# Which engine folds the attention output, and in how many pieces, in a fused attention, Fourier mixing and MLP kernel on one core

## The chip, the cores and the metric

The kernel runs on one core of one Trainium2 chip. The metric is the device time of one execution in microseconds (us), as the median of three runs. The core's engines are TensorE (PE in the trace; PEld are its weight loads), VectorE (DVE), ScalarE (ACT), GpSimd (POOL) and SyncE (SP), which issues the DMAs. Each works through its own queue in order and waits on semaphores for the others.

## What is computed

Four batches of 768 tokens pass through three blocks. The first is a gated linear attention with 8 heads of 48; its output, 768 x 384 per batch, gets a two-dimensional Fourier transform, whose real part is added, a normalisation and an MLP; then come a token-mixing MLP and a second channel MLP.

```python
# attention, per batch and head
for t in range(S):
    S_re, S_im = ar * S_re - ai * S_im + kv, ar * S_im + ai * S_re
    y[:, :, t] = einsum('bhd,bhde->bhe', q[:, :, t], S_re)
# block 1
mixed = real(fft(fft(x, axis=1), axis=2))
u = x + mixed
un = (u - mean(u)) / sqrt(var(u) + 1e-6)
x = u + relu(un @ w_ch1) @ w_ch2
# block 2
u = x + (relu(x.T @ w_tok1) @ w_tok2).T
out = u + relu(u @ w_ch1) @ w_ch2
```

## The kernel before

**Two streams.** The work on a batch has a chain part (the attention, `stage1`, and the Fourier mixing, `stage2`, with many short operations on all engines) and a dense part (the two MLPs and the token mixing: matmuls of 128 x 128 by 128 x 384). The kernel writes the chain of batch b+1 beside the dense part of batch b. A scheduler puts both into one order per engine when the kernel is built, by priorities (`RANK`) and its own estimate of times; on the chip these orders are fixed. Only the first batch's chain (beside which the weights are converted, L191 to L206) and the last two batches' dense part have no such partner.

**The end of the attention.** `stage1` works through 8 chunks of 96 tokens. For each, TensorE does L753 (scores), L768 and L769 (state), L802 and L808 (output), and ScalarE writes the chunk's 96 columns of the tile `xT` (L810). L808 and L753 read the tile `qkt`, of the pool tag "qk", which has one buffer of 12288 columns.

**The folds.** `stage2` folds `xT`, 112 x 4 x 768, for a Fourier transform that uses symmetries. L982 adds and subtracts columns n and 384 + n (xm and xp), so a piece of columns needs chunk k and chunk k + 4. L988 adds and subtracts the halves of xm and xp (four results xd). L999 adds or subtracts each xd and its mirror image, for four types `ty` of transform and two halves r (eight results fd); it needs whole rows of 384. In batches 2 to 4 (b = 1 to 3) xm, xp, xd and fd lie in `ws`, which is again of the tag "qk"; in the first batch xm, xp and xd lie elsewhere. Then ScalarE copies the edge columns (L1006), TensorE multiplies by cosines and sines (L1022, two matmul records for each in the trace), ScalarE copies to Z (L1024), TensorE does the second transform (L1033), and the rows are joined, normalised and transposed (L1080, L1085 to L1114, L906 to L910).

**Who folds.** `XP` gives the pieces (start, width) of a batch: four of 96 in the first batch, one of 288 and one of 96 in the others. `PD` names the xd results that GpSimd makes (in later batches xd[1][1]), `PF` the fd results that GpSimd makes in later batches (type 2, both halves). xp is always GpSimd's, the rest VectorE's. In front of a later batch's folds stand, in VectorE's queue, the last L760 and the dense part's operations; between them the scheduler puts dense ones: L932 (the MLP's rectified hidden, from PSUM) and L945 (adds the MLP's output to u, from PSUM). TensorE's dense matmuls, L926 (first MLP matrix) and L942 (second), write PSUM tiles of tag "l", of which there are three: a tile is free again when L932 or L945 has read it. One quarter of an MLP is six groups of nine L926, then six groups of nine L942.

Of the kernel before, what the change touches and what calls it, by code (L numbers as in the profile page):

```python
# [34 lines left out]
AH = 4  # L35
KS, EN = 5, 3
OFF = ((2, 3), 1, 0)
XP = [((0, 96), (96, 96), (192, 96), (288, 96))] + [((0, 288), (288, 96))] * 4
NR = [((0, 192),)] * 5
KT, PF, PD = (0, 1), ((2, 0), (2, 1)), (((1, 0), (1, 1)), ((1, 1),))  # L40
O = (0, 1, 0)
HOLD = mybir.DependencyInfo(mybir.DependencyClass.NoSync, mybir.DependencyReason.SCHED_ONLY)
CHK_A, CHK_E = 6.0e4, 1.0e-7
# [10 lines left out]
def attn_fft_mixer_kernel(ctx: ExitStack, tc: tile.TileContext, aL, xL, vL, wL, qN, kN, vN, arN, aiN,  # L54
# [18 lines left out]
    ve, se, ge = Prio(nc.vector, "v"), Prio(nc.scalar, "v"), Prio(nc.gpsimd, "v")  # L73
# [18 lines left out]
    def alloc(tag, shape, dt=F32, name=None):  # L92
        n = 1
        for x in shape[1:]:
            n *= x
        t = pool.tile([128, SIZE[tag]], dt, tag=tag, bufs=BUFS[tag], name=name or tag)
        return shaped(t[0:shape[0], 0:n], shape)
# [37 lines left out]
    xT = pool.tile([112, 4, S], F32, name="xT")  # L135
# [29 lines left out]
    def after(x, y):  # L165
        tc.add_manual_dep(x.ins, y.ins.name, HOLD, reason="order of the streams")
# [138 lines left out]
    def warm(n, x):  # L305

        ps = palloc("l", [128, 512])
        for _ in range(n):
            te.matmul(out=ps[:, 0:x.shape[1]], lhsT=ident[0:x.shape[0], :], rhs=x)
# [644 lines left out]
    def stage2(b):  # L954
        space = alloc("qk", [128, 12288], name="ws")
        def part(name, pat=None, **kw):
            o, n = WSP[name]
            v = space[:, o:o + n]
            return v.rearrange(pat, **kw) if pat else v
# [6 lines left out]
        if b == 0:  # L966

            xm, xp = (alloc("h", [112, 4, 384], name="xf") for _ in range(2))
            xd = alloc("h", [112, 4, 384], name="xd")
            xd = [[xd[:, 0:2], xd[:, 2:4]], [alloc("tmp", [112, 2, 384], name="xd") for _ in range(2)]]  # L970
        else:
            xf = part("xf", "p (a b) -> p a b", a=8)[0:112]
            xm, xp = xf[:, 0:4, :], xf[:, 4:8, :]
            xd = part("xd", "p (s r a b) -> p s r a b", s=2, r=2, a=2)[0:112]
            xd = [[xd[:, s, r] for r in range(2)] for s in range(2)]
        fd = part("fd", "p (t r a b) -> p t r a b", t=4, r=2, a=2)[0:112]
        Z = part("Z", "p (a b) -> p a b", a=8)
        for k, (o, n) in enumerate(XP[b]):
            n += o
            an = None if b or AN[k] is None else free[AN[k]]  # L980
            for s, x, op in ((0, xm, ALU.subtract), (1, xp, ALU.add)):
                x1 = (ge if s else ve).tensor_tensor(out=x[:, :, o:n], in0=xT[:, :, o:n], in1=xT[:, :, 384 + o:384 + n], op=op)  # L982
                if an is not None:
                    after(x1, an)
                if b == 0 and k == 3 and s == 0:
                    warm(1, xm[:, 0, :])
                for r, op2 in enumerate((ALU.add, ALU.subtract)):
                    x1 = (ge if (s, r) in PD[b > 0] else ve).tensor_tensor(out=xd[s][r][:, :, o:n], in0=x[:, 0:2, o:n], in1=x[:, 2:4, o:n], op=op2)  # L988
                    if an is not None:
                        after(x1, an)  # L990
                    if b == 0 and k == 3 and s == 0:
                        warm(1, xd[0][r][:, 0, :])

        kinds = ((0, 0, ALU.subtract, 0, 191), (1, 0, ALU.add, 1, 192), (2, 1, ALU.add, 0, 192), (3, 1, ALU.subtract, 1, 191))
        for n0, n1 in NR[b]:
            for ty, s, op, f0, f1 in kinds:
                lo, hi, sh = max(n0, f0, 1), min(n1, f1, 191) + 1, ty % 2
                for r in range(2):
                    x = (ge if (ty, r) in PF and b else ve).tensor_tensor(out=fd[:, ty, r, :, lo - sh:hi - sh], in0=xd[s][r][:, :, lo:hi],  # L999
                                                                in1=xd[s][r][:, :, 384 - lo:384 - hi:-1], op=op)  # L1000
                    if b == 0 and ty < 2:
                        warm(1, fd[:, ty, r, 0, 1:191])
                for n in (0, 192):
                    if n0 <= n <= n1 and f0 <= n <= f1:
                        for r in range(2):
                            se.copy(out=fd[:, ty, r, :, n - sh:n - sh + 1], in_=xd[s][r][:, :, n:n + 1])  # L1006
# [9 lines left out]
        for kt in KT:  # L1016
            for ty in range(4):
                n0, n = 128 * kt, ZK[ty][kt]
# [37 lines left out]
        for i in range(3):  # L1056
# [19 lines left out]
            for half in range(2):  # L1076
# [10 lines left out]
                lo, hi = (1, 2) if half == 0 else (2, 1)  # L1087
# [111 lines left out]
    def chain(b):  # L1199
        stage1(b)  # L1200
        return stage2(b)
# [28 lines left out]
    with tc.If(fv != 0):  # L1230
        with tc.For_i(0, B, 1) as b:
            fallback(b)
            u, norm = stage2(B)
            t = transposed(u, norm, "s")
            dense2(B, u, *dense1(B, u, *t), row=b)
# [111 lines left out]
```

## Time and profile before

| | |
|---|---|
| median of three runs (lowest to highest) | 1103.9 us (1103.21 to 1104.33) |
| profiled execution | 1103.4 us, of which its span 1101.6 us |
| mean granted clock of TensorE over the span | 0.955 |
| busy: TensorE, VectorE, ScalarE, GpSimd | 985.5, 784.3, 506.2, 387.3 us |

The span reaches from the first to the last instruction of the profiled execution; all places in it are us from its start. A granted clock of 1.00 is 2.4 GHz, 0.50 is 1.2 GHz. A row of the timeline merges instructions of one kind that follow each other (x27); its time reaches from the first one's start to the last one's end, and since an instruction starts shortly before the one ahead of it ends, the distance from start to start is less than a duration. In square brackets stands how long the engine was idle before the row and what ended that.

### The profile page before, as it was taken

What the parts mean: (1) busy time and instruction counts of PE and PEld (TensorE: products, weight loads), DVE (VectorE), ACT (ScalarE), POOL (GpSimd) and SP (SyncE); (2) the same over time, 40 slices, a digit from 0 to 9 for tenths busy, and PEclk for the clock granted to TensorE, in tenths of its full rate; (3) what the DMA queues carried; (4) which work ended last, traced back from release to release, by engine and by line L of the source; (5) the groups of instructions that cost most, each with busy time, mean ns of one, the idle gap of its engine ahead of it and who ended that gap; (6) DMA issues with size and microseconds to landing.
All of it is one profiled execution on the core that took longest, in us unless ns stands there. A gap on an engine that the chain in (4) does not pass through costs nothing.

```text
span 1101.6 us, 21033 instructions
## 1 busy us (share of the span) xinstructions
PE 985.5 (89%) x7314; PEld 923.1 (84%) x7314; DVE 784.3 (71%) x2115; ACT 506.2 (46%) x1393; POOL 387.3 (35%) x520
## 2 busy tenths in 40 slices
PE   1368887999889999799998999999986999999997
PEld 0237775989788888699998899999976999999997
DVE  6986987999999668999767879985555433433332
ACT  6753355777876225867423567751124112121111
POOL 6643985573576444223226312211432002000000
PEclk9987797999999998899998999999988999999999
DMA  6137954686758664355565336655412433443432
GB/s 215 45 82 179 293 176 154 209 283 194 231 179 278 194 178 135 99 168 185 179 160 172 112 112 193 205 161 146 139 48 66 151 115 129 158 151 130 165 101 74
DMA packets 101536, 174.65 MB, mean 159 GB/s; under 512 B 11056, under 2 KB 61104, under 8 KB 100912
## 3 DMA queue, kind: packets, MB, share of 16 engines
q1 hardware_dynamic: 101424, 173.24, 51.1%
q8 instruction: 60, 0.98, 0.4%
q14 instruction: 52, 0.43, 0.1%
HBM read 133.88 MB, written 39.32 MB: 157 GB/s over the span
## 4 chain that ended last, share of the span: by engine, by line
PE 65%; DVE 10%; DMA 2%; ACT 1%; issue 1%; POOL 1%; SPq 0%; POOLq 0%; DVEq 0%; ACTq 0%
PE l L942 24%; PE l L926 22%; PE s L753 3%; PE s L642 2%; PE s L1033 2%; PE s L1022 2%; PE s L802 2%; DMA cvt<-wL 2%; PE s L808 1%; PE s L1147 1%; DVE ws L982 1%; PE s L1165 1%; PE s L768 1%; DVE cvt L199 1%; PE s L906 1%
## 5 line engine op out<-in xcount | busy, mean ns | idle before, releaser
L942 PE MATMUL l<-w,h 128*128 128x384 f32 x1728 | 332.5, 345 | 12.1 <-DVE h L932 8.4
L926 PE MATMUL l<-th,w 128*128 128x384 f32 x1152 | 314.4, 342 | 5.1 <-DVE h L932 2.6
L942 PEld LDWEIGHTS l<-w,h 128*128 128x128 f32 x1728 | 304.4, 192 | 16.8 <-DVE h L932 11.6
L926 PEld LDWEIGHTS l<-th,w 128*128 128x128 f32 x1152 | 210.8, 190 | 9.1 <-DVE h L932 4.1
L930 ACT ACTIVATE h<-l 128x384 fp32r<-128x384 f32 x192 | 94.0, 490 | 225.3 <-PE l L926 224.8
L926 PE MATMUL l<-tl,w 128*128 128x384 f32 x576 | 195.3, 339 | 0.0
L932 DVE SCALAR_TENSOR_TENSOR h<-l,h 128x384 fp32r<-128x384 f32 x192 | 106.2, 553 | 88.3 <-ACT h L930 87.9
L945 DVE TENSOR_TENSOR u<-u,l 128x384 f32<-128x384 f32 x192 | 105.4, 550 | 76.0 <-PE l L942 75.1
L926 PEld LDWEIGHTS l<-tl,w 128*128 128x128 f32 x576 | 109.1, 189 | 0.4 <-issue 0.2
L196 POOL TENSOR_TENSOR cvt<-cvt 128x384 int32<-128x384 int32 x56 | 64.8, 1163 | 38.2 <-DVE cvt L194 9.4
L466 PE MATMUL s<-misc,y 128*112 128x128 f32 x96 | 22.1, 377 | 52.1 <-DVE y L444 48.6
L753 PE MATMUL s<-qkt 112*96 112x96 f32 x512 | 59.7, 267 | 8.0 <-DVE sc L760 7.9
L466 PEld LDWEIGHTS s<-misc,y 128*112 128x112 f32 x96 | 14.5, 181 | 61.9 <-issue 27.3
L753 PEld LDWEIGHTS s<-qkt 112*96 112x96 f32 x512 | 53.4, 177 | 11.1 <-DVE sc L760 8.7
L786 POOL TENSOR_TENSOR yc<-Aa,gm 48x384 f32<-48x384 f32 x18 | 21.0, 1165 | 100.8 <-DVE Aa L779 100.8
L206 POOL TENSOR_TENSOR w<-cvt,w 128x384 fp32r<-128x384 f32 x44 | 51.1, 1170 | 10.5 <-ACT w L205 7.0
L199 DVE SCALAR_TENSOR_TENSOR cvt<-cvt 128x384 int32<-128x384 int32 x56 | 48.8, 878 | 7.0 <-POOL cvt L196 6.8
L1132 POOL TENSOR_TENSOR xl<-u,xh 128x384 fp32r<-128x384 f32 x18 | 17.9, 1004 | 101.1 <-ACT xh L1131 101.1
L571 POOL TENSOR_TENSOR tm<-tm 128x144 f32<-128x144 f32 (+1 forms) x51 | 26.6, 523 | 73.7 <-ACT tm L570 73.7
L642 PE MATMUL s<-misc,y 128*112 128x128 f32 x288 | 45.7, 275 | 1.5 <-DVE y L626 1.0
L615 DVE TENSOR_TENSOR p<-p,A 128x144 f32<-128x144 f32 x144 | 44.7, 310 | 2.0
L589 POOL TENSOR_TENSOR A<-raw,tm 128x144 f32<-128x144 f32 (+1 forms) x51 | 26.1, 513 | 56.0 <-DVE tm L587 29.4
(232 smaller groups left out, 1905.3 us busy)
## 6 DMA issues: line engine op xcount, KB each, us to landing
w<-wscr SPq DMA_DIRECT2D x180, 384.0 KB, 3.5
cvt<-wL SPq DMA_DIRECT2D x56, 384.0 KB, 4.7
wscr<-w SPq DMA_DIRECT2D x44, 384.0 KB, 3.2
Kn<-kn SPq DMA_DIRECT2D x64, 192.0 KB, 3.8
kn<-y SPq DMA_DIRECT2D x96, 96.0 KB, 2.7
raw<-aL SPq DMA_DIRECT2D x48, 144.0 KB, 3.0
xx<-xL SPq DMA_DIRECT2D x48, 144.0 KB, 3.2
V<-vL SPq DMA_DIRECT2D x32, 144.0 KB, 3.3
```

Of the source, the lines that this page charges most:

```text
L196: x = ge.tensor_tensor(out=a, in0=a, in1=lo, op=ALU.add)
L199: rest(ve.scalar_tensor_tensor(out=a, in0=hi, scalar=-0x80000000, in1=a, op0=ALU.bitwise_and, op1=ALU.bitwise_or))
L206: ge.tensor_tensor(out=parts[:, 1, :], in0=a.bitcast(F32), in1=r32(parts[:, 0, :]), op=ALU.subtract)
L466: te.transpose(ps[:, j, :], y[:, j, 0:112], ident)
L615: ve.tensor_tensor(out=cur, in0=prev, in1=A[:, j, 0:3, :], op=ALU.mult)
L642: te.transpose(ps[:, j, :], y[:, j, 0:112], ident)
L753: te.matmul(out=ps[:, j, :], lhsT=K[:, hc, :], rhs=Q[:, hc, :])
L926: te.matmul(out=ps, lhsT=w1[:, wi, kt * 128:kt * 128 + 128], rhs=x[g][:, kt, :], start=(n == 0), stop=(n == 8))
L930: x = se.activation(out=hi, in_=ps, func=ACTF.Relu)
L932: ve.scalar_tensor_tensor(out=h[:, 1, g * 384:g * 384 + 384], in0=ps, scalar=0.0, in1=r32(hi), op0=ALU.max, op1=ALU.subtract)
L942: te.matmul(out=ps, lhsT=hs[m][:, hi, tt * 128:tt * 128 + 128], rhs=w2[:, wi, :], start=(n == 0), stop=(n == 8))
L945: ve.tensor_tensor(out=u[tt], in0=u[tt], in1=ps, op=ALU.add)
```

## The change

All batches get four pieces of 96 columns. GpSimd makes xp, and the xd results that `PD` names, only for the first three of them (k < 3), in the first batch as well; the fourth piece is VectorE's alone. `PF` is gone: all L999 run on VectorE.

```diff
--- before.py
+++ after.py
@@ -35,9 +35,9 @@
 AH = 4
 KS, EN = 5, 3
 OFF = ((2, 3), 1, 0)
-XP = [((0, 96), (96, 96), (192, 96), (288, 96))] + [((0, 288), (288, 96))] * 4
+XP = [((0, 96), (96, 96), (192, 96), (288, 96))] * 5
 NR = [((0, 192),)] * 5
-KT, PF, PD = (0, 1), ((2, 0), (2, 1)), (((1, 0), (1, 1)), ((1, 1),))
+KT, PD = (0, 1), (((1, 0), (1, 1)), ((1, 1),))
 O = (0, 1, 0)
 HOLD = mybir.DependencyInfo(mybir.DependencyClass.NoSync, mybir.DependencyReason.SCHED_ONLY)
 CHK_A, CHK_E = 6.0e4, 1.0e-7
@@ -979,13 +979,13 @@
             n += o
             an = None if b or AN[k] is None else free[AN[k]]
             for s, x, op in ((0, xm, ALU.subtract), (1, xp, ALU.add)):
-                x1 = (ge if s else ve).tensor_tensor(out=x[:, :, o:n], in0=xT[:, :, o:n], in1=xT[:, :, 384 + o:384 + n], op=op)
+                x1 = (ge if s and k < 3 else ve).tensor_tensor(out=x[:, :, o:n], in0=xT[:, :, o:n], in1=xT[:, :, 384 + o:384 + n], op=op)
                 if an is not None:
                     after(x1, an)
                 if b == 0 and k == 3 and s == 0:
                     warm(1, xm[:, 0, :])
                 for r, op2 in enumerate((ALU.add, ALU.subtract)):
-                    x1 = (ge if (s, r) in PD[b > 0] else ve).tensor_tensor(out=xd[s][r][:, :, o:n], in0=x[:, 0:2, o:n], in1=x[:, 2:4, o:n], op=op2)
+                    x1 = (ge if k < 3 and (s, r) in PD[b > 0] else ve).tensor_tensor(out=xd[s][r][:, :, o:n], in0=x[:, 0:2, o:n], in1=x[:, 2:4, o:n], op=op2)
                     if an is not None:
                         after(x1, an)
                     if b == 0 and k == 3 and s == 0:
@@ -996,7 +996,7 @@
             for ty, s, op, f0, f1 in kinds:
                 lo, hi, sh = max(n0, f0, 1), min(n1, f1, 191) + 1, ty % 2
                 for r in range(2):
-                    x = (ge if (ty, r) in PF and b else ve).tensor_tensor(out=fd[:, ty, r, :, lo - sh:hi - sh], in0=xd[s][r][:, :, lo:hi],
+                    x = ve.tensor_tensor(out=fd[:, ty, r, :, lo - sh:hi - sh], in0=xd[s][r][:, :, lo:hi],
                                                                 in1=xd[s][r][:, :, 384 - lo:384 - hi:-1], op=op)
                     if b == 0 and ty < 2:
                         warm(1, fd[:, ty, r, 0, 1:191])
```

In the order that the scheduler makes, three places show it. First VectorE in the fourth batch (b = 3), beside the dense part of the third: L760 ends the attention, u_65.. are the token tiles of the dense part. Before:

```order
L760 TENSOR_TENSOR sc<-s,misc 96x384 x2
L932 SCALAR_TENSOR_TENSOR h<-l,h 128x384
L982 TENSOR_TENSOR ws<-xT 112x4x288
L982 TENSOR_TENSOR ws<-xT 112x4x96
L988 TENSOR_TENSOR ws<-ws 112x2x288 x2
L945 TENSOR_TENSOR u_6503<-u_6503,l 128x384
L988 TENSOR_TENSOR ws<-ws 112x2x96 x2
L988 TENSOR_TENSOR ws<-ws 112x2x288
L945 TENSOR_TENSOR u_6504<-u_6504,l 128x384
L988 TENSOR_TENSOR ws<-ws 112x2x96
L999 TENSOR_TENSOR ws<-ws 112x2x191 x4
```

With the change:

```order
L760 TENSOR_TENSOR sc<-s,misc 96x384
L945 TENSOR_TENSOR u_6516<-u_6516,l 128x384
L760 TENSOR_TENSOR sc<-s,misc 96x384
L982 TENSOR_TENSOR ws<-xT 112x4x96 x3
L988 TENSOR_TENSOR ws<-ws 112x2x96 x2
L945 TENSOR_TENSOR u_6517<-u_6517,l 128x384
L982 TENSOR_TENSOR ws<-xT 112x4x96 x2
L988 TENSOR_TENSOR ws<-ws 112x2x96 x6
L945 TENSOR_TENSOR u_6518<-u_6518,l 128x384
L988 TENSOR_TENSOR ws<-ws 112x2x96 x5
L945 TENSOR_TENSOR u_6519<-u_6519,l 128x384
```

Two of the six L945 of this MLP quarter now stand ahead of the folds (u_6515 and u_6516, the second one just ahead of these rows' L982), and the next behind three L982 and two L988; all eight L999 come after the last L945.

Second, TensorE at the same place, from the last L808 of the batch's attention to the first L1033 (an L1022 here is two records of the trace). Before:

```order
L808 MATMUL s<-qkt,T 48x96
L942 MATMUL l<-w,h 128x384 x45
L1022 MATMUL s<-dcos,ws 128x97 x12
L942 MATMUL l<-w,h 128x384 x9
L1022 MATMUL s<-dcos,ws 128x97 x4
L1022 MATMUL s<-dcos,ws 64x97 x8
L1022 MATMUL s<-dcos,ws 65x97 x4
L1022 MATMUL s<-dcos,ws 63x97 x4
L1033 MATMUL s<-ws 128x193 x4
```

With the change:

```order
L808 MATMUL s<-qkt,T 48x96
L942 MATMUL l<-w,h 128x384 x31
L1022 MATMUL s<-dcos,ws 128x97 x16
L1022 MATMUL s<-dcos,ws 64x97 x8
L1022 MATMUL s<-dcos,ws 65x97 x4
L1022 MATMUL s<-dcos,ws 63x97 x4
L1033 MATMUL s<-ws 128x193 x4
```

Behind the last L808 stand 31 dense L942 instead of 54, and none between the L1022.

Third, VectorE in the second batch (b = 1), beside the dense part of the first. Before:

```order
L932 SCALAR_TENSOR_TENSOR h<-l,h 128x384
L982 TENSOR_TENSOR ws<-xT 112x4x288
L982 TENSOR_TENSOR ws<-xT 112x4x96
L988 TENSOR_TENSOR ws<-ws 112x2x288 x2
L932 SCALAR_TENSOR_TENSOR h<-l,h 128x384
L988 TENSOR_TENSOR ws<-ws 112x2x96 x2
L945 TENSOR_TENSOR u_1512<-u_1512,l 128x384
L988 TENSOR_TENSOR ws<-ws 112x2x288
L999 TENSOR_TENSOR ws<-ws 112x2x191
L945 TENSOR_TENSOR u_1513<-u_1513,l 128x384
L988 TENSOR_TENSOR ws<-ws 112x2x96
L999 TENSOR_TENSOR ws<-ws 112x2x191 x3
```

With the change:

```order
L932 SCALAR_TENSOR_TENSOR h<-l,h 128x384
L982 TENSOR_TENSOR ws<-xT 112x4x96 x3
L988 TENSOR_TENSOR ws<-ws 112x2x96 x2
L982 TENSOR_TENSOR ws<-xT 112x4x96 x2
L988 TENSOR_TENSOR ws<-ws 112x2x96 x5
L932 SCALAR_TENSOR_TENSOR h<-l,h 128x384
L988 TENSOR_TENSOR ws<-ws 112x2x96 x6
L932 SCALAR_TENSOR_TENSOR h<-l,h 128x384
L945 TENSOR_TENSOR u_1512<-u_1512,l 128x384
L999 TENSOR_TENSOR ws<-ws 112x2x191 x4
L577 SCALAR_TENSOR_TENSOR tm<-tm 128x144
L999 TENSOR_TENSOR ws<-ws 112x2x191 x4
```

Two L932 now stand between the folds, the first behind five L982 and seven L988, instead of one behind two L982 and two L988 of 288 columns.

On GpSimd a later batch's folds were two L982 (288 and 96 columns), two L988 and two L999; they become three L982 and three L988 of 96 columns.

## Rows read from the trace of the kernel before

**Rows 1.** Page, first part: busy us (share of the span) and instructions by engine.
```profile
PE 985.5 (89%) x7314; PEld 923.1 (84%) x7314; DVE 784.3 (71%) x2115; ACT 506.2 (46%) x1393; POOL 387.3 (35%) x520
```

**Rows 2.** Timeline of VectorE, fourth batch: start, us, group, count, idle before and its releaser.
```profile
794.90 4.31 DVE L982 TENSOR_TENSOR ws<-xT 112x1152 f32<-112x1152 f32 x2 [1.65 <-PE s L808]
...
805.69 2.76 DVE L999 TENSOR_TENSOR ws<-ws 112x382 f32<-112x382 f32 x4
...
808.83 1.01 DVE L999 TENSOR_TENSOR ws<-ws 112x382 f32<-112x382 f32 x2
```

**Rows 3.** Timeline of TensorE, fourth batch.
```profile
794.44 0.34 PE L808 MATMUL s<-qkt,T 112*48 112x96 f32 x4
794.70 4.95 PE L942 MATMUL l<-w,h 128*128 128x384 f32 x27
803.08 6.03 PE L942 MATMUL l<-w,h 128*128 128x384 f32 x18 [3.42 <-DVE u L945]
808.94 2.82 PE L1022 MATMUL s<-dcos,ws 112*128 112x97 f32 x24
...
813.19 4.13 PE L1022 MATMUL s<-dcos,ws 112*128 112x97 f32 x40
817.25 2.16 PE L1033 MATMUL s<-ws 128*128 128x193 f32 x8
```

**Rows 4.** Chain that ended last, last dense stretch: start, us, group, count.
```profile
884.63 9.36 PE l L942 x54
```

**Rows 5.** Stretches of the fourth batch: busy by engine, granted clock, DMA share, GB/s.
```profile
803.00:809.00 6.00, 5.92 (x19) 5.93 (x20) 6.00 (x12) 2.73 (x10) 2.32 (x3) 0.51 0.00 0
809.00:811.00 2.00, 2.00 (x20) 2.00 (x19) 1.77 (x4) 0.32 (x2) 0.00 (x0) 1.00 0.03 8
```

**Rows 6.** Timeline of TensorE, second and third batch.
```profile
407.29 3.29 PE L942 MATMUL l<-w,h 128*128 128x384 f32 x18
413.60 6.13 PE L942 MATMUL l<-w,h 128*128 128x384 f32 x18 [3.02 <-DVE h L932]
...
596.77 2.55 PE L942 MATMUL l<-w,h 128*128 128x384 f32 x8 [2.07 <-DVE h L932]
600.29 3.57 PE L942 MATMUL l<-w,h 128*128 128x384 f32 x10 [0.97 <-DVE h L932]
```

**Rows 7.** Groups by line and shape, fourth batch: busy us, mean ns, idle before.
```profile
L982 POOL TENSOR_TENSOR ws<-xT 112x1152 f32<-112x1152 f32 x1 | 3.8, 3832 | 3.7 <-PE s L808 3.7
...
L982 DVE TENSOR_TENSOR ws<-xT 112x384 f32<-112x384 f32 x1 | 3.0, 3034 | 0.0
...
L999 POOL TENSOR_TENSOR ws<-ws 112x382 f32<-112x382 f32 x2 | 2.3, 1154 | 1.8 <-DVE ws L988 1.7
L988 POOL TENSOR_TENSOR ws<-ws 112x576 f32<-112x576 f32 x1 | 1.9, 1913 | 0.0
...
L982 DVE TENSOR_TENSOR ws<-xT 112x1152 f32<-112x1152 f32 x1 | 1.4, 1359 | 1.6 <-PE s L808 1.6
L982 POOL TENSOR_TENSOR ws<-xT 112x384 f32<-112x384 f32 x1 | 1.3, 1317 | 0.0
...
L1006 ACT COPY ws<-ws 112x2 f32<-112x2 f32 x8 | 1.2, 193 | 0.5 <-DVE ws L999 0.3
L988 POOL TENSOR_TENSOR ws<-ws 112x192 f32<-112x192 f32 x1 | 1.1, 1106 | 0.0
```

**Rows 8.** Timeline of VectorE, first batch.
```profile
140.97 1.01 DVE L982 TENSOR_TENSOR xf<-xT 112x384 f32<-112x384 f32 x2
141.91 1.15 DVE L988 TENSOR_TENSOR xd<-xf 112x192 f32<-112x192 f32 x4
144.57 0.86 DVE L982 TENSOR_TENSOR xf<-xT 112x384 f32<-112x384 f32 x1 [1.51 <-ACT xT L810]
...
146.69 5.42 DVE L999 TENSOR_TENSOR ws<-xd 112x382 f32<-112x382 f32 x8
```

**Rows 9.** Durations by line, GpSimd's forms of the first batch: min/median/max ns.
```profile
L982 POOL TENSOR_TENSOR xf<-xT x4: 1123/1742/2969, 132.5 to 146.5; 112x384 f32<-112x384 f32 x4
...
L988 POOL TENSOR_TENSOR xd<-xf x8: 587/745/901, 137.1 to 148.5; 112x192 f32<-112x192 f32 x8
```

## The prediction

> **What bounds the kernel now.** I read the page's busy times first: TensorE works 89% of the span [rows 1], so the time is TensorE's work plus its stops plus what it loses at its lower clock. Then I looked for stops where the change lies: in the stretches where a batch's attention output xT is folded for the Fourier mixing (L982, L988, L999) while TensorE goes on with dense matmuls of the batch before. In the fourth batch the folds start at 794.90 [rows 2]. TensorE runs 27 dense L942, stands 3.42 us until VectorE's addition L945 frees a PSUM tile, and needs 6.03 us for the next 18 [rows 3], which at the rate of 54 in 9.36 us [rows 4] take 3.1. The granted clock is 0.51 in that stretch, that is 1.2 GHz, and 1.00, 2.4 GHz, behind it [rows 5]. One stop has cost 3.4 + 2.9 = 6.3 us. The second batch shows the same, 3.02 us and 6.13 for 18; in the third there are two shorter stops, 2.07 and 0.97 [rows 6]. They are no lack of work: L945 and L932, which would free PSUM tiles, stand behind folds in VectorE's queue.
>
> Two more things are read there. First, **the folds do not wait for their chunk**. Their output "ws" and the "qkt" that L808 reads share one buffer (tag qk, one copy), and the first fold follows an idle stretch that L808 ended [rows 2], whose last group began at 794.44 [rows 3]. Second, **VectorE and GpSimd take turns**. VectorE's 288-wide piece takes 1.36 us; GpSimd's, freed by the same L808, takes 3.83; VectorE's 96-wide piece then takes 3.03 [rows 7], where such a piece takes 0.54 alone [rows 8]. That is 1.28 for VectorE, then 2.55 for GpSimd, then 0.47: a sum, nothing in parallel.
>
> **The change, part by part.** *Earlier folds in batches 2 to 4:* nothing. The first piece still writes into qkt's buffer, so it waits for the same L808.
>
> *Work moved.* Start to start, an operation on VectorE takes 0.47 us at 384 or 382 elements and 0.27 at 192 (two take 1.01, four 1.15) [rows 8]; by the same slope 1.28 at 1152 and 0.67 at 576. VectorE's share of a later batch was 1.28 + 0.47 + 3 x 0.67 + 3 x 0.27 + 6 x 0.47 = 7.4; it becomes 5 x 0.47 + 13 x 0.27 + 8 x 0.47 = 9.6. GpSimd's was 2.55 + 0.9 + 1.25 + 0.5 + 2 x 0.9 = 7.0 (durations [rows 7], each less what VectorE held of it); it becomes 3 x 0.9 + 3 x 0.5 = 4.2, at most 3 x 1.12 + 3 x 0.59 = 5.1 by the shortest of its two forms [rows 9]. **Saved per batch: 0.6 us**, where the two collide throughout (none, if they hold it for the 5.1). For the fourth batch before, 7.4 + 7.0 and three L945 of 0.47 make 15.8; 794.90 to 809.84 [rows 2] is 14.9, since GpSimd does not hold up an L945. After: 9.6 + 4.2 + 4 x 0.47 less the same 0.9 is 14.8. The phase ends where it ended; its first pair of L999, for which TensorE's L1022 waits, ends 6 x 0.47 earlier, 12.0 after the first fold.
>
> *The order.* The queues are fixed when the kernel is built, and the changed folds make the scheduler place dense work elsewhere. Counted in TensorE's order ahead of the last L808, batch 2 has 865 dense matmuls instead of 876, batch 3 has 1494 instead of 1473, batch 4 has 2273 instead of 2250. What is done ahead of the folds is missing as cover beside them. So I count stops and clock loss, not start times.
>
> *Batch 4, the largest term.* 31 L942 remain. At 9.36/54 = 0.173 us, 22 take 3.8; the next needs the addition that now stands behind three L982 and two L988: 3 x 0.47 + 2 x 0.27 + 3 x 0.9 + 0.47 = 5.1. Stop of 1.3, nine more by 6.7. Then no dense work is left; TensorE stands until the first pair is there (12.0) and ScalarE has copied its edges (two of 0.19 [rows 7]): 5.7 us. The 64 L1022 take 2.6 + 4.1 = 6.7 us at full rate [rows 3] and lose something at 1.2 GHz: 0 at best, 6.7 if all ran so. I take 2.4, next to the 2.9 that the 3.42 us stop cost. Lost: 1.3 + 5.7 + 2.4 = 9.4 against 6.3, **+3.1** (ends +0.7 and +7.4). From here to the end all engines have the order of before.
>
> *Batch 2.* 17 L926 and 8 L942 take 4.3; then L942 needs an L932 that stands behind 5 L982 and 7 L988: 2.35 + 1.9, GpSimd's 4.2, itself 0.47: 8.9; 8.0 if two of GpSimd's come later. A stop of 4.6 or 3.7 instead of 3.02, with the same loss in clock behind it: **+0.9** (+0.7 to +1.6). In front of VectorE's queue there, two L932 and an L945 wait for folds; TensorE alone waits for them.
>
> *Batch 3.* Before: 3.0 of stops, and 18 L942 in 2.55 + 3.57 instead of 3.1 [rows 6]: 6.0. After: 27 L942 cover 4.7; the addition that is needed then comes behind 5 L982 and 5 L988, 3.7 + 4.2 + 0.5 = 8.4. Stop 3.7, and 3.0 at the lower clock: +0.7. If VectorE holds on through a run, as at 140.97, where a piece of GpSimd took 2.97 us while six VectorE folds passed [rows 8, 9], the addition comes near 6.7, the stop is 2.0, and with no clock loss that is -4. I lean on the first, since at this very place in three batches GpSimd had its turn after one fold, but shade it: **+0.3**.
>
> *Batch 1.* In its fourth quarter 0.9 + 2 x 0.5 leave GpSimd, 0.47 + 2 x 0.27 come to VectorE: 145.43 + 2 x 0.45 of GpSimd's rest + 0.47 + 4 x 0.27 + 8 x 0.47 = 151.6 for the last L999, where it was 146.69 + 5.42 = 152.1 [rows 8]. **-0.6**, or 0 if the weight conversions behind it (L196, L199) take it up.
>
> Sum: -0.6 + 3.1 + 0.9 + 0.3 = +3.7. The profiled execution took 1103.4 us (its span 1101.6 and 1.8 around it), so 1107.1; the median is 0.5 above it: **1107.6**. The measurement can tell about 0.2%, 2.2 us, from no change.
>
> **The rivals.** *Fewer turns pay, and it is faster.* GpSimd's longest hold falls from 2.55 to 0.9, so L945 and L932 may come early enough that TensorE hardly stops in batches 2 and 3. For it: a stop of 3 us costs 3 more in clock, so a small gain spares 6. If both go that way, -0.6 - 5 - 4 + 3.1 = -6.5, 1097.4. Against it: the additions now stand behind seven to thirteen folds instead of four to eight. It decides from the point where these stops fall under 2 us.
>
> The Trainium skill (SBUF — State Buffer, "SBUF: two separate sides") says that VectorE and GpSimd share a port pair as an exclusive lock, which whoever starts first holds for the whole instruction. By that rule the turns above agree, and each batch gains what the sums of holds show, 0.6; four times 0.6 would give 1101.5.
>
> *It washes out.* The phases are equally long (14.9 and 14.8), and batch 4 loses little clock: +0.7 there, and the others cancel: 1102 to 1106, near 1104.
>
> *The lost cover costs its far end.* In batch 4 the Fourier matmuls run wholly at 1.2 GHz behind a stop of 5.7 us: +7.4 for +3.1, 1111.9. It decides when that stop exceeds the 3.42 of before.
>
> **How the numbers follow.** The forecast with its far end (over 1106.1): 0.55. The wash: 0.28. Turns that pay (under 1101.7): 0.17. The range leaves out the far ends of first and last: 1101.0 to 1111.5.
>
> **What would show it.** Right: the first fold of batches 2 to 4 still directly behind the last L808; a fold phase of batch 4 near 14.8 us; a TensorE stop of 5 to 6 us ahead of its L1022, with a clock of 0.5 behind it; its L1033 near 821 instead of 817.25. Wrong: a first fold ahead of the last L808; stops under 2 us in batches 2 and 3; VectorE folding in runs while GpSimd waits.

## The result, and the profile after

The changed kernel takes **1115.58 us** (1114.90 to 1116.19 in four runs) against 1103.56 for the kernel before on the same chip: ratio 1.0110, 95% interval [1.0093, 1.0128]. It is slower, as forecast, but by 12 us and not by 4; 1111.5 was the upper end of the range. Here and below a ratio is to the kernel before on the same chip; the experiments ran on several chips. The profiled execution took 1116.19 us, with a span of 1114.3 against 1101.6.

First part of its page: busy us, share of the span, instructions.
```profile
PE 989.2 (89%) x7314; PEld 926.5 (83%) x7314; DVE 786.6 (71%) x2154; ACT 505.3 (45%) x1393; POOL 374.3 (34%) x517
```
Against [rows 1] GpSimd lost 13 us of work and VectorE took 2 more. That is the change as written, and it says nothing about where 12.7 us went. For that I set the two TensorE timelines beside each other by one thing that both do in the same amount: the dense matmuls (L926, L942, L1147, L1165), counted from the start. The start of the 55th lies behind the first batch's folds, that of the 973rd behind the second's, of the 2101st behind the third's, and the last of 3744 behind the fourth's. After minus before it is +5.0, +7.7, +7.6 and +12.8 us. So the batches cost **+5.0, +2.7, 0 and +5.2**, where the forecast had -0.6, +0.9, +0.3 and +3.1 (each from one execution: where the queues are the same, the first fold of all starts anywhere from 131.04 to 132.51, so about 1.5 us of such a difference can be chance); and the fourth batch's first L1033, which the forecast put near 821, starts at 830.14.

At the folds themselves the trace shows nearly what was worked out. TensorE's timeline of the changed kernel in the second, third and fourth batch (start, us, group, count, idle before and its releaser):
```profile
418.04 7.07 PE L942 MATMUL l<-w,h 128*128 128x384 f32 x28 [4.59 <-DVE h L932]
...
610.71 7.74 PE L942 MATMUL l<-w,h 128*128 128x384 f32 x27 [3.70 <-DVE u L945]
...
806.62 4.09 PE L942 MATMUL l<-w,h 128*128 128x384 f32 x22
812.23 1.83 PE L942 MATMUL l<-w,h 128*128 128x384 f32 x9 [1.52 <-DVE u L945]
818.67 11.54 PE L1022 MATMUL s<-dcos,ws 112*128 112x97 f32 x64 [4.61 <-ACT ws L1006]
830.14 2.16 PE L1033 MATMUL s<-ws 128*128 128x193 f32 x8
```
The stops were forecast at 4.6, 3.7, 1.3 and 5.7; they are 4.59, 3.70, 1.52 and 4.61. The last is 1.1 shorter than forecast: the 31 L942 ended 7.4 us behind their start and not 6.7, and the L1022 began 12.05 behind it and not 12.4. The last row but one is new against [rows 3]: 64 L1022 in one piece take 11.54 us where 24 and 40 took 2.82 and 4.13. VectorE's side of the same stretch:
```profile
806.82 3.14 DVE L982 TENSOR_TENSOR ws<-xT 112x384 f32<-112x384 f32 x3 [1.65 <-PE s L808]
...
817.79 3.81 DVE L999 TENSOR_TENSOR ws<-ws 112x382 f32<-112x382 f32 x8
```
The first fold still follows L808, and the fold phase runs from 806.82 to 821.60: 14.8 us, as worked out.

The first batch holds the surprise. VectorE's timeline there, to be read beside [rows 8]:
```profile
139.73 1.01 DVE L982 TENSOR_TENSOR xf<-xT 112x384 f32<-112x384 f32 x2
...
146.46 3.81 DVE L999 TENSOR_TENSOR ws<-xd 112x382 f32<-112x382 f32 x8
```
From the first of these rows to the last fold this is 10.5 us, where it was 140.97 to 152.11, 11.1: the -0.6 of the forecast is there (the whole batch also began 1.2 us earlier in this execution). And yet the first dense matmul behind this batch starts 5.0 us late. Two things lie between. First the clock (windows: busy by engine, then granted clock, DMA share, GB/s). The stretch from the first L1033 on in the kernel before:
```profile
162.00:176.00 14.00, 12.70 (x71) 8.78 (x70) 10.06 (x28) 5.68 (x17) 11.87 (x15) 1.00 0.61 229
```
and in the changed kernel:
```profile
160.00:176.00 16.00, 15.06 (x50) 10.30 (x50) 11.07 (x29) 4.92 (x15) 11.96 (x14) 0.59 0.56 206
```
The granted clock is 1.00 (2.4 GHz) there before and 0.59 after: it fell to 1.2 GHz at 162.8, with no stop of TensorE over 0.65 us in the 12 us ahead. Second, a stop that the kernel before has at less than half the size. TensorE before:
```profile
184.06 1.51 PE L906 MATMUL s<-misc,ws 128*128 128x128 f32 x6 [2.50 <-DVE ws L1114]
```
and after:
```profile
189.81 1.51 PE L906 MATMUL s<-misc,ws 128*128 128x128 f32 x6 [6.39 <-DVE ws L1114]
```
VectorE in front of that L1114, before:
```profile
182.58 0.15 DVE L1104 TENSOR_TENSOR rs<-rs 128x2 f32<-128x2 f32 x1
...
183.36 0.16 DVE L1108 SCALAR_TENSOR_TENSOR rs<-mv,rs 128x2 f32<-128x2 f32 x1
183.44 0.47 DVE L1114 TENSOR_SCALAR ws<-u,mv,rs 128x384 f32<-128x384 f32 x1
183.83 0.35 DVE L194 TENSOR_SCALAR cvt<-cvt 128x384 int32<-128x384 int32 x1
```
and after:
```profile
184.89 0.36 DVE L194 TENSOR_SCALAR cvt<-cvt 128x384 int32<-128x384 int32 x1 [0.36 <-ACT cvt L191]
185.42 1.00 DVE L1104 TENSOR_TENSOR rs<-rs 128x2 f32<-128x2 f32 x1 [0.17 <-ACT rs L1102]
...
186.73 0.36 DVE L194 TENSOR_SCALAR cvt<-cvt 128x384 int32<-128x384 int32 x1
187.01 0.15 DVE L1107 TENSOR_TENSOR rs<-rs 128x2 f32<-128x2 f32 x1
187.08 0.55 DVE L199 SCALAR_TENSOR_TENSOR cvt<-cvt 128x384 int32<-128x384 int32 x1
187.55 0.97 DVE L1108 SCALAR_TENSOR_TENSOR rs<-mv,rs 128x2 f32<-128x2 f32 x1
188.44 1.23 DVE L1114 TENSOR_SCALAR ws<-u,mv,rs 128x384 f32<-128x384 f32 x1
```
None of these is a fold. The builder has put steps of the weight conversions (two L194 and an L199) into the chain of small normalisation steps that TensorE waits for, on ScalarE as well (L191 and L192 between L1101 and L1102). From L1104 to the end of L1114 it takes 4.25 us, where it took 1.33. With a conversion comes its GpSimd half, and beside that the 2-element steps take up to 1.00 us instead of 0.15:
```profile
185.39 1.02 POOL L196 TENSOR_TENSOR cvt<-cvt 128x384 int32<-128x384 int32 x1 [6.44 <-ACT rs L1102]
```
L1104 ends at 186.42 and this L196 at 186.41. The Trainium skill (SBUF — State Buffer, "SBUF: two separate sides") gives VectorE and GpSimd one port pair, locked for a whole instruction; these rows agree with it, and show a tiny operation held for as long as a large one.

So the theory to test: **the folds cost about what was forecast, and the rest comes from queues**, which the builder lays out anew for every kernel when the folds change.

### The profile page after: what moved, and what is told of

It reads as the page before. It is cut to its first block, busy times and chain, and to the rows that moved or that the text cites. A ratio compares the mean times of both kernels' runs of the same rounds, so it can differ in the third digit from the quotient of the medians.

```text
span 1114.3 us, 21060 instructions
## 1 busy us (share of the span) xinstructions
PE 989.2 (89%) x7314; PEld 926.5 (83%) x7314; DVE 786.6 (71%) x2154; ACT 505.3 (45%) x1393; POOL 374.3 (34%) x517
## 4 chain that ended last, share of the span: by engine, by line
PE 68%; DVE 19%; DMA 4%; issue 3%; ACT 3%; POOL 2%; SPq 0%; POOLq 0%; DVEq 0%; ACTq 0%
PE l L926 22%; PE l L942 22%; PE s L753 3%; PE s L1033 3%; PE s L1022 2%; PE s L642 2%; PE s L802 2%; DVE cvt L199 2%; PE s L808 1%; DVE ws L982 1%; PE s L1147 1%; PE l L1165 1%; PE s L1165 1%; PE s L768 1%; DVE ws L988 1%
## 5 line engine op out<-in xcount | busy, mean ns | idle before, releaser
L942 PE MATMUL l<-w,h 128*128 128x384 f32 x1728 | 325.5, 341 | 11.7 <-DVE h L932 6.5
L926 PE MATMUL l<-th,w 128*128 128x384 f32 x1152 | 316.8, 344 | 4.9 <-DVE h L932 3.6
L942 PEld LDWEIGHTS l<-w,h 128*128 128x128 f32 x1728 | 302.5, 191 | 14.1 <-DVE h L932 7.9
L926 PEld LDWEIGHTS l<-th,w 128*128 128x128 f32 x1152 | 211.4, 190 | 9.3 <-DVE h L932 6.6
L926 PE MATMUL l<-tl,w 128*128 128x384 f32 x576 | 195.7, 340 | 0.0
L932 DVE SCALAR_TENSOR_TENSOR h<-l,h 128x384 fp32r<-128x384 f32 x192 | 106.3, 553 | 93.4 <-ACT h L930 92.7
L945 DVE TENSOR_TENSOR u<-u,l 128x384 f32<-128x384 f32 x192 | 105.1, 549 | 69.8 <-PE l L942 68.9
L926 PEld LDWEIGHTS l<-tl,w 128*128 128x128 f32 x576 | 109.6, 190 | 0.5 <-DVE tl L910 0.3
L196 POOL TENSOR_TENSOR cvt<-cvt 128x384 int32<-128x384 int32 x56 | 64.6, 1158 | 39.0 <-DVE cvt L194 11.9
L199 DVE SCALAR_TENSOR_TENSOR cvt<-cvt 128x384 int32<-128x384 int32 x56 | 44.6, 804 | 5.3 <-POOL cvt L196 5.0
```

Source lines behind the costliest of these rows:

```text
L196: x = ge.tensor_tensor(out=a, in0=a, in1=lo, op=ALU.add)
L199: rest(ve.scalar_tensor_tensor(out=a, in0=hi, scalar=-0x80000000, in1=a, op0=ALU.bitwise_and, op1=ALU.bitwise_or))
L926: te.matmul(out=ps, lhsT=w1[:, wi, kt * 128:kt * 128 + 128], rhs=x[g][:, kt, :], start=(n == 0), stop=(n == 8))
L932: ve.scalar_tensor_tensor(out=h[:, 1, g * 384:g * 384 + 384], in0=ps, scalar=0.0, in1=r32(hi), op0=ALU.max, op1=ALU.subtract)
L942: te.matmul(out=ps, lhsT=hs[m][:, hi, tt * 128:tt * 128 + 128], rhs=w2[:, wi, :], start=(n == 0), stop=(n == 8))
L945: ve.tensor_tensor(out=u[tt], in0=u[tt], in1=ps, op=ALU.add)
```

## The experiments

**Parts of the change, alone.** The first four kernels undo or do one part and let the builder lay out the queues. With the first batch folded as before:
```diff
-(ge if s and k < 3 else ve)
+(ge if s and (k < 3 or b == 0) else ve)
-(ge if k < 3 and (s, r) in PD[b > 0] else ve)
+(ge if (k < 3 or b == 0) and (s, r) in PD[b > 0] else ve)
```


> The changed kernel with the first batch folded as before (fourth quarter shared with GpSimd again); the later batches keep the change. By milestones of the two traces the 12 us came as about +5 in the first batch, +3 in the second, +0 in the third and +5 in the fourth. Theory 1 (each batch's loss comes from where its dense matmuls and weight conversions stand in the fixed queues, and the first batch's part sets those of all later batches too): here the conversions L194 and L199 stand behind the first batch's last L1114 again, and 51 dense L942 instead of 31 stand between the last L808 and the first L1022 of the fourth batch. The first batch's +5.0 goes, and of the fourth's +5.1 nearly all goes: 1103.6 + 2.7 = 1106, range 1103 to 1108, with a TensorE stop under 3 us ahead of the fourth batch's L1022. Theory 2 (each batch's loss belongs to its own new folds): only the first batch's +5.0 goes, 1110.6. Theory 3 (the clock in the first batch fell by accident, not by the order): 1115.

Measured (e1) 1104.51, ratio 1.0013 [1.0001, 1.0026]. The later batches' whole change costs a tenth of the difference; the time is in theory 1's range, and the additive one (1110.6) is out. And the reverse, the kernel before with the first batch's part alone:
```diff
-(ge if s else ve)
+(ge if s and (k < 3 or b) else ve)
-(ge if (s, r) in PD[b > 0] else ve)
+(ge if (k < 3 or b) and (s, r) in PD[b > 0] else ve)
```


> The kernel before with only the first batch's part of the change (its fourth quarter folded on VectorE alone). VectorE's queue between the first batch's last joins L1085 and its last L910 is that of the changed kernel, two L194 and one L199 ahead of the last L1114. Theory 1: the first batch loses about 5.0, made of 2.4 gained up to its first L1033, 5.0 lost from L1033 to the first L906 at a granted clock of 0.5, and 2.4 lost ahead of the last L906; 51 dense L942 instead of 45 in front of the fourth batch's L1022 change little: 1108.6, range 1106 to 1111. My forecast on record gave the first batch -0.6: 1103. Theory 3 (the low clock was an accident): no low clock from L1033 on, 1103.6 - 2.4 + 2.4 = 1103.6.

Measured (e2) 1115.06, ratio 1.0111 [1.0092, 1.0131]: three folds moved in the first batch cost all of it, and more than theory 1 allowed (1106 to 1111). The profiled execution (1111.3; the other three, 1114.5 to 1116.2, have no trace) puts the loss where my split by batches did not have it: the four milestones are 0.0, +3.5, +7.9 and +8.1. Its first batch has the conversions in the chain and the stop that goes with them:
```profile
184.83 1.51 PE L906 MATMUL s<-misc,ws 128*128 128x128 f32 x6 [7.06 <-DVE ws L1114]
```
It lost nothing all the same, because its first L1033 came 3.1 us earlier than before (159.66; 1.9 of that stands already at the first fold of all) and the granted clock from 160 to 176 was 0.89, not 0.59. In the third batch's scan TensorE stands for a load:
```profile
553.78 0.23 PE L768 MATMUL s<-V,Kn 96*64 96x48 f32 x1 [2.81 <-DMA Kn<-kn]
```
That stop is in neither the kernel before nor the changed one. So a part's cost is not a fixed sum over places; each build has its own.

The mirror folds alone:
```diff
-(ge if (ty, r) in PF and b else ve)
+ve
```


> The kernel before with all mirror folds L999 on VectorE, and nothing else of the change. The first two batches keep the queues of before ahead of the fold; 44 L942 stand between the last L808 and the first L1022 of the fourth batch instead of 45. By the sums of holds VectorE gets 2 x 0.47 more in each later batch and GpSimd holds 2 x 0.9 less: the fold phases are 0.9 shorter. Theory 1 and theory 2: within 2 us of before, 1101 to 1105; first pair of L999 not earlier, so the fourth batch's stop ahead of L1022 does not grow. If fewer turns of GpSimd were what pays or costs most, 1097 to 1100.

Measured (e3) 1108.86, ratio 1.0066 [1.0039, 1.0093], with executions from 1106.8 to 1117.5: outside what any theory had given. It is a small move of work that again came with other queues. In its profiled execution (1107.32, below the median) the third batch costs 2.6 us: TensorE waits 1.69 for the load of Kn at the same place, and the stop at the fold is 4.14 instead of 2.07 and 0.97. The longest executions have no trace.

The quarters alone:
```diff
-XP = [((0, 96), (96, 96), (192, 96), (288, 96))] + [((0, 288), (288, 96))] * 4
+XP = [((0, 96), (96, 96), (192, 96), (288, 96))] * 5
```


> The kernel before with quarters in the later batches, GpSimd's share of the folds kept. Its longest hold falls from 2.55 to 0.9 us, its number of turns grows. 42 L942 stand between the last L808 and the first L1022 of the fourth batch, 54 L942 in the third, 51 dense in the second. Theory 1 (cover decides): the second batch's stop is 4 to 5 us, the fourth batch is within 2 us of before since its cover is 42 instead of 45: 1103.6 + 1 to 3, 1104.5 to 1107. Theory 2 (the folds themselves cost): VectorE's additions stand behind more folds, so each of the three later batches loses 2 to 5: 1109 to 1115. First fold of each batch directly behind the last L808 in either.

Measured (e4) 1106.35, ratio 1.0022 [1.0008, 1.0036], within theory 1; the second batch's stop is 4.81, where 4 to 5 was expected. The parts do not add up to the whole: 1.0111, 1.0066 and 1.0022 against 1.0110 together.

**Folds and queues apart.** The next four kernels take the queues out of the builder's hands. From the other built program I took the order of every instruction on every engine, and put an ordering edge (no wait, no semaphore) between neighbours on one engine; only the folds L982, L988, L999 are left free. In the traces of these kernels VectorE's and ScalarE's instructions other than folds stand, by line and shape, in the order that was asked for, without exception, and so do the DMAs that SyncE issues:
```diff
+    for names in ORDER():                 # one list for each engine
+        was = None
+        for n in names:
+            x = by.get(f"I-{n}")
...
+            if was is not None and was.engine == x.engine:
+                tc.add_manual_dep(x, was.name, HOLD, reason="order of the queues")
+            was = x
```
The queues of the kernel before, with all folds of the change:

> All folds of the change, but every other instruction of every engine stands in the order that the kernel before has (ordering edges that add no wait; the folds themselves, L982, L988 and L999, stand where the builder puts them). So the first batch's conversions L194 and L199 are behind its last L1114 again, and 42, 39 and 45 dense matmuls stand between the last L808 and the first L1022 of the later batches. Theory Q (the loss is in the queues that the new folds made the builder lay out): within 3 us of before, 1101 to 1107. Theory F (the loss is in the folds, their engines and sizes): 1112 to 1116.

Measured (e5) 1108.16, ratio **1.0035** [1.0022, 1.0049], that is +3.9 us; the milestones of the profiled execution (1106.21, one of the four shortest of nine) are -0.9, +1.4, +3.1 and +3.0. This is slightly above theory Q's range and far from theory F's. At the last L906 of the first batch the stop is 2.50 again. The folds of before, with the queues of the changed kernel:

> No fold of the change: the kernel before, its folds as they were, but every other instruction of every engine in the order of the changed kernel: conversions ahead of the first batch's last L1114, 53, 54 and 31 dense matmuls in front of L1022. Theory Q: 1112 to 1117, of which the first batch +2 to +8 (the stop ahead of its last L906 near 6 us, the low clock from L1033 on as it may fall), the fourth +4 to +6 with a TensorE stop of 4 to 6 us ahead of its L1022. Theory F: 1101 to 1106.

Measured (e6) 1117.52, ratio **1.0132** [1.0108, 1.0157], milestones +3.6, +7.6, +8.0 and +14.6. Not one fold has another engine or size, and the kernel is as slow as the changed one, or slower (theory Q's range ended at 1117). Its rows are those of the changed kernel, the stop ahead of the last L906 and the one ahead of L1022:
```profile
188.42 1.51 PE L906 MATMUL s<-misc,ws 128*128 128x128 f32 x6 [6.38 <-DVE ws L1114]
...
819.83 11.97 PE L1022 MATMUL s<-dcos,ws 112*128 112x97 f32 x64 [5.91 <-ACT ws L1006]
```
The first batch's part alone, in the queues of before:

> The first batch's part alone, three folds moved from GpSimd to VectorE, with every other instruction in the order of the kernel before. The same folds in the queues that they made the builder lay out took 1115.1. Theory Q: the forecast on record for this part, -0.6, up to the -2.4 that the changed kernel's trace shows at the first batch's first L1033: 1101 to 1103.5. Theory F: 1112 to 1116.

Measured (e7) 1104.89, ratio 1.0010 [0.9993, 1.0026], against 1.0111 for the same folds in their own queues. It is no gain either, and 1.4 us above theory Q's range: the first dense matmul comes 1.3 us early, and the 973rd 0.1. Last, the folds of before in the queues of the first-batch kernel:

> The folds of before with every other instruction in the order of the kernel that has the first batch's part alone (which took 1115.1). Theory Q: 1111 to 1116, with no fold moved at all. Theory F: 1101 to 1106.

Measured (e8) 1113.19, ratio 1.0098 [1.0075, 1.0121], again with no fold moved. Its profile repeats the wait for Kn, 3.21 us up to 553.61, so that stop belongs to those queues.

Read together, these four leave the queues as the larger part. With the old folds the changed kernel's queues cost 14.6 us (1.0132); with the new folds they cost 8.3 (1.0110 against 1.0035). The new folds cost 3.9 in the old queues and nothing that can be told in their own (1.0110 against 1.0132, intervals that overlap). So the two prices do not add up, and 14.6 is not the share of the queues in the 12. No kernel was run with the edges alone; those with edges in the old queues came out at 1.0010 (e7) and 1.0015 (e10, below), so the edges do not explain 8 or 14 us. What the builder derives from an order, its semaphores for one, goes with the order and was not taken apart from it.

**What the clock costs.** Two kernels keep TensorE busy in a stop with matmuls whose product nobody reads, all else in the queues of its base. In the changed kernel:
```diff
+        if b in WB: warm(WB[b], ident, "s")      # WB = {3: 18}
         for kt in KT:
```


> The changed kernel in its own queues, with 18 matmuls of 128 x 128 whose product nobody reads put into TensorE's queue between the fourth batch's last L942 and its first L1022, where it stands 4.61 us (such a matmul takes 0.22 at the full rate by the first batch's rows, 18 take 4.0). Theory C (the granted clock falls because TensorE stands, and the 64 L1022 lose 4.7 us by it: 11.5 instead of 6.8): the clock stays at 1.00, the L1022 take about 7, 1110 to 1112. Rival (the clock falls at this place anyway): the 18 run at half rate too, the L1022 take 11 or more and begin later: 1115 to 1119.

Measured (e9) 1111.39, ratio 1.0073 [1.0044, 1.0102] against 1.0110 [1.0093, 1.0128], in theory C's range; the intervals overlap a little, so the rows must tell. TensorE's timeline, and the window behind the stop in the changed kernel and in this one:
```profile
813.58 4.18 PE L309 MATMUL s<-misc 128*128 128x128 f32 x36
818.33 2.50 PE L1022 MATMUL s<-dcos,ws 112*128 112x97 f32 x20 [0.57 <-ACT ws L1006]
821.07 4.68 PE L1022 MATMUL s<-dcos,ws 112*128 112x97 f32 x44 [0.25 <-ACT ws L1006]
```
```profile
818.00:828.00 10.00, 9.33 (x46) 9.16 (x47) 3.60 (x8) 3.44 (x14) 0.00 (x0) 0.51 0.01 2
```
```profile
818.00:828.00 10.00, 9.43 (x74) 7.90 (x75) 3.26 (x7) 3.94 (x18) 0.00 (x0) 1.00 0.00 1
```
The 18 matmuls (two records each) fill the stop, the clock stays at 1.00, and from the first L1022 to the first L1033 (825.69) it is 7.4 us instead of 11.5: 4.1 less. Theory C holds there. In the kernel before, with `WB = {1: 12, 2: 8, 3: 14}` and these matmuls queued in front of the first matmul behind each stop:

> The kernel before in its own queues, with matmuls that nobody reads in TensorE's three main stops beside the folds: 12 in the second batch's (3.02 us), 8 in the third's first (2.07), 14 in the fourth's (3.42). Behind these the dense matmuls lost about 3.0, 2 and 2.9 us at 1.2 GHz. Theory C: no low clock there, 1095 to 1099, faster than before. Rival (the clock falls anyway): the matmuls take twice as long and run past the ends of the stops, 1104 to 1110.

Measured (e10) 1103.62, ratio 1.0015 [0.9997, 1.0033], between the two ranges: no gain, though the clock did stay up in these windows. The windows of the second and fourth batch before:
```profile
412.00:420.00 8.00, 6.40 (x23) 6.40 (x23) 8.00 (x12) 3.86 (x11) 6.06 (x7) 0.57 0.49 159
803.00:809.00 6.00, 5.92 (x19) 5.93 (x20) 6.00 (x12) 2.73 (x10) 2.32 (x3) 0.51 0.00 0
```
and here:
```profile
412.00:420.00 8.00, 6.76 (x41) 6.19 (x40) 8.00 (x12) 3.91 (x13) 6.05 (x7) 1.00 0.23 78
802.00:808.00 6.00, 4.97 (x30) 4.14 (x29) 6.00 (x11) 2.34 (x7) 3.01 (x3) 1.00 0.00 0
```
In both kernels VectorE is busy for all of these windows. The dense matmuls run twice as fast and then wait for the same additions, in the second batch for example:
```profile
412.44 1.84 PE L942 MATMUL l<-w,h 128*128 128x384 f32 x9 [0.35 <-DVE h L932]
415.06 1.86 PE L942 MATMUL l<-w,h 128*128 128x384 f32 x9 [0.78 <-DVE u L945]
```
The Trainium skill (TensorE: Matmul & The Clock Gate, "Terms") puts the penalty of a low clock at its time by one half; with the granted clocks above, 8 x 0.43 + 6 x 0.49, that is an estimate of 6.4 us for these two windows. The run gave none of it, and the measurement decides.

**The conversions of the first batch.** In the changed kernel's own queues, the conversions that stand ahead of the last L1114 (on ScalarE: of the last L1112) come behind it. VectorE's order there:
```diff
-VectorE: L194 L1104 L1105 L1106 L194 L1107 L199 L1108 L1114 L199 L910 L910
+VectorE: L1104 L1105 L1106 L1107 L1108 L1114 L194 L194 L199 L199 L910 L910
```


> The changed kernel in its own queues with one exchange in the first batch: on VectorE the two L194 and the L199 that stand ahead of the last L1114 come right behind it, and on ScalarE the L191, L192 and L205 that stand ahead of the last L1112 behind that, as in the kernel before. Theory Q: the stop of 6.39 us ahead of the first batch's last L906 shrinks to about 3.3, first dense matmuls 3 us earlier, and if nothing gives it back 1112 to 1113. Rival (the stop comes from the low clock and late joins, not from the conversions): the stop stays over 5.5, 1115 to 1116; given back later in the second batch: stop 3.3, but 1115.

Measured (e11) 1114.30, ratio 1.0103 [1.0077, 1.0130]: not told apart from the changed kernel. The stop at L906 fell to 2.76, but one of 4.57 came ahead of the first L926, for which the L909 behind the conversions had to run. So the exchange was made complete, with the conversions in the places of before on both engines:
```diff
+VectorE: L1104 L1105 L1106 L1107 L1108 L1114 L194 L199 L194 L910 L910 L199
-ScalarE: L1101 L191 L192 L1102 L191 L192 L205 L1112 L558 L558 L205 L909 L567 L909 L567
+ScalarE: L1101 L1102 L191 L192 L1112 L558 L558 L191 L192 L909 L909 L205 L567 L205 L567
```


> The changed kernel in its own queues, with the weight conversions around the end of the first batch in the places that they have in the kernel before, on VectorE and on ScalarE: one L191/L192 pair ahead of the last L1112 and one behind, both L205 behind the last L909, one L194 and L199 behind the last L1114 and one L199 behind the last L910. The exchange before this one moved the 6.39 us stop from the last L906 to the first L926 (4.57, for the th that L909 stood with behind both L205), so nothing was gained. Theory Q: neither stop now; from the last aggregate L1093 to the first L926 about 5 us as in the kernel before instead of 7.2, dense matmul 54 at +2 to +3 instead of +4.8 to +5.0 against before, and if nothing gives it back 1112.5 to 1113.5. Rival (it is given back by the end of the second batch): dense matmul 54 early, but 972 at +7 to +8 as before, 1114 to 1116.

Measured (e12) 1114.08, ratio 1.0099 [1.0080, 1.0119]. The rows are as expected:
```profile
184.01 1.51 PE L906 MATMUL s<-misc,ws 128*128 128x128 f32 x6 [2.76 <-DVE ws L1114]
186.18 0.69 PE L926 MATMUL l<-th,w 128*128 128x384 f32 x1 [0.65 <-ACT th L909]
```
The first dense matmul comes where it came before (186.18 against 186.23), instead of 5.0 us later. But the 55th is at +3.1 and the 973rd at +6.4, and the end at +11.3 instead of +12.8: most is given back, as the rival said, and the rest (1.5) is within what these runs can tell. The time, too, lies in the rival's range (1114 to 1116).

## Why the prediction was right, and where it failed

*What held.* The direction; three of the four stops beside the folds (4.59, 3.70 and 1.52 us); the fold phase of 14.8 us; the first batch's folds 0.6 us shorter (the sum in the forecast, 151.6 against 152.11, gives 0.5); folds that start behind the last L808; no gain from fewer turns of GpSimd. The forecast of +3.7 is close to what the new folds cost in queues that do not move, +3.9 [2.4 to 5.4], but that is luck: its terms counted the cover in the new queues. With the old queues the first batch gains 0.9, the second and third lose 2.2 and 1.7 (forecast +0.9 and +0.3) behind stops of 4.77 and 5.02, and the fourth, which has 45 L942 of cover again, loses nothing (forecast +3.1 for 31). That split is of an execution 2 us below the median.

*What failed: the step called "The order", with "So I count stops and clock loss, not start times".* It saw that the builder had placed dense work elsewhere, and costed the new queues only as cover beside the folds. For the first batch it had "-0.6, or 0 if the weight conversions behind it take it up" and no term for a conversion that moves into another chain. The runs showed that the new queues cost 8.3 us with the new folds in place and 14.6 with every fold as before. In the changed kernel the loss shows in three places.
- First batch, +5.0 instead of -0.6. From the first L1033 to the first dense matmul it takes 23.4 us before and 30.9 after. It takes 26.6 in the profile of e9, whose queues up to here are the same but where the clock fell at 179.5 instead of 162.8, 26.6 in that of e2, and 24.8 in that of e12, which moves the conversions back. So about 3 us are the conversions in the chain (in stops, 6.39 against e12's 2.76 and 0.65), about 4 the early fall of the clock, and 2.4 were gained up to the first L1033. The clock's part belongs to one execution: in e9 the 55th dense matmul is at +2.2.
- Second batch, +2.7 instead of +0.9. At the fold the stop grew by 1.57, the upper end of the forecast. Three stops of the tail grew by 1.28 in sum; before and after:
```profile
445.17 1.54 PE L906 MATMUL s<-misc,ws 128*128 128x128 f32 x6 [4.37 <-ACT ws L1112]
448.50 1.54 PE L906 MATMUL s<-misc,ws 128*128 128x128 f32 x6 [1.79 <-DVE p L617]
450.58 1.54 PE L906 MATMUL s<-misc,ws 128*128 128x128 f32 x6 [0.53 <-ACT ws L1112]
```
```profile
451.18 1.54 PE L906 MATMUL s<-misc,ws 128*128 128x128 f32 x6 [5.05 <-ACT ws L1112]
454.00 1.54 PE L906 MATMUL s<-misc,ws 128*128 128x128 f32 x6 [1.28 <-ACT ws L1112]
457.18 1.54 PE L906 MATMUL s<-misc,ws 128*128 128x128 f32 x6 [1.64 <-ACT ws L1112]
```
They go with the queues: e6 has 5.04, 1.28 and 1.64, and e5, with all folds of the change, 4.38, 1.79 and 0.53. What each would be worth was not tried, and the returned gain of e12 says that they can't be added up. Nor does the line between the first two batches hold from execution to execution: in e9 and e11 the 55th is at +2.2 and +4.8, and the 973rd at +7.5 and +7.4.
- Fourth batch, +5.2 instead of +3.1. Here the mechanism was right and sizes were off: the stop ahead of L1022 (5.7 for 4.61) and, more, the clock. I put 2.4 on the L1022 after and 2.9 on the dense matmuls before. e9 gives 4.1 for the first; for the second e10 gives at most 1.5 (its first L1033 of this batch starts at 815.73, against 817.25 in [rows 3]). With these, 1.52 + 4.61 + 4.1 against 3.42 + 1.5 is +5.3, and +5.2 was measured. The loss goes with the cover: with the changed folds, 31, 45 and 51 L942 between the last L808 and the first L1022 cost +5.2 (after), -0.1 (e5) and -1.5 (e1) in this batch; 42 and 44 cost +1.1 (e4) and +1.2 (e3), and the old folds with 31 cost +6.6 (e6).

*The rivals.* The far end of the lost cover had the right mechanism for the fourth batch, with 7.4 where 5.2 was measured, and stayed at 1111.9 because the first two batches were missing. Turns that pay are refuted by e5. The wash is refuted by the result.

*What stays open.* Why the clock falls at 162.8 in one execution and later in another is not shown, nor why moving the conversions back (e12) gained nothing at the end, nor what makes e3's longest executions, up to 1117.5, so long. No version here is faster than the kernel before; e7 and e10 are the nearest, at 1.0010 and 1.0015.

## What to carry to other kernels

Where a builder lays out the queues, an edit has two prices: its own work, and the new order of everything else, which here was two to four times as large (8.3 and 14.6 us against 3.9). They need not add up. Compare the whole order of each engine, not the edited place, and look for foreign work that has moved into a chain of small steps (here 3 us at the place, though little of it was left at the end); then measure the two apart by building the new work in the old order and the old work in the new. Time at the lower clock is a loss only where nothing else bounds the work behind it: it cost 4.1 us where the input of the matmuls behind the stop was complete, and at most 1.5 where they had to wait for VectorE.

## What the runs showed of the hardware that was not expected

A VectorE operation on 128 x 2 elements, 0.15 us alone, took 1.00 beside GpSimd's conversion add of 1.02 us. Eighteen matmuls without use kept the granted clock at 1.00 across a stop of 4.6 us. And the granted clock fell to one half at 162.8 in a stretch in which TensorE was 9.59 of 10 us busy:
```profile
150.00:160.00 10.00, 9.59 (x89) 8.97 (x88) 9.10 (x13) 4.79 (x15) 9.38 (x7) 1.00 0.01 2
160.00:170.00 10.00, 9.64 (x31) 6.53 (x32) 6.64 (x10) 3.02 (x9) 9.99 (x11) 0.64 0.60 237
```
(windows of the changed kernel; the seventh number is the granted clock).
